# A 128-byte load of W1 rows on ScalarE's queue and a regenerated order, in a fused FFT filter and MLP kernel

## The chip, the cores and the metric

The kernel runs on one core of a Trainium2 chip. The metric is the device time of one execution in microseconds. The kernel before has a median of 148.31 us over three runs, 148.28 to 148.42. All times inside the kernel come from one profiled execution; they count from the start of its span.

## The reference

A batch of one, 2048 rows of 640 values in bf16. The rows are layer-normalized once (xn), and the output is the sum of three terms: x itself, a global filter on xn (a real 2-D FFT, a product with complex weights, the inverse FFT), and a two-layer MLP on xn with a tanh-approximated GELU.

```python
def _A_ref(x, w_r, w_i):
    X = rfft2(x.astype(float32), axes=(-2, -1))
    X = X * (w_r + 1j * w_i)
    return irfft2(X, s=(S, D), axes=(-2, -1)).astype(bfloat16)
def _B_ref(x, w1, b1, w2, b2):
    h = gelu(einsum("bsd,df->bsf", x, w1) + b1)
    return einsum("bsf,fd->bsd", h, w2) + b2
xn = layernorm(x)
return x + _A_ref(xn, A_w_r, A_w_i) + _B_ref(xn, B_w1, B_b1, B_w2, B_b2)
```

S is 2048, D is 640, F (the hidden width) is 1536.

## The kernel before

**Order and synchronization.** The kernel records its work as numbered operations (`Sched.op`), each with what it reads and writes. A long text, `ORDER`, gives for every operation its place and engine (s SyncE, p TensorE, a ScalarE, d VectorE, g GpSimd) and, behind a colon, the buffer slots it takes: `258p:0` is operation 258 on TensorE in slot 0. `arrange` reads that text, and `sync` works out which operation must wait for which, and leaves out waits that follow from others. Each engine then runs its own operations strictly in that order, so an operation that waits holds up everything behind it on its engine. The times written beside the operations (`at=...` for the arrival of a load, in us) are those with which the text was made; the program on the chip contains only the order. An operation keeps the number in which it was recorded, so one more operation shifts the numbers of all later ones by one.

**Loads.** Every load goes through `load`, whose DMA instruction stands at L375. SyncE's queue carries the large ones in this order: the rows of x for chunk 0 and chunk 1 (a chunk is 128 of the 2048 rows, every sixteenth), then W1 in five row blocks of 128 rows by 1536 columns (L433 to L436, 384 KB each; block j holds the weights of the j-th 128 of the 640 inputs) with chunks 2 and 3 of x between the third and the fourth, then the FFT table `gtab` (L437), the other chunks of x in pairs, b2 and W2. ScalarE's queue first loads the table of the square root, then issues the load of b1 (L432), then runs the square root of the first chunk's variance (L489), and loads the table of the GELU (L490). Its later loads come after 21 us.

**Head.** For each chunk VectorE computes statistics (L483, L485), the reciprocal root is made (L489 and L491 for chunk 0, GpSimd at L494 for the others), and VectorE normalizes (L513). Chunks 0 to 3 are transposed by TensorE (L531) and copied out of PSUM to xnT by VectorE and ScalarE (L394, L395); later chunks go through DMA transposes. Until its first input is ready TensorE multiplies zeros (L409, 40 matmuls). The first layer of the MLP begins with chunks 0 and 1 together: six tiles of hidden units (b = 0 to 5, L570 on), each a sum over the five row blocks of W1. In the first three row blocks the two chunks have matmuls of their own, 128 wide, recorded in pairs (two halves of a tile); in the last two they go together, 256 wide. All matmuls have one source line, L383, since a helper issues them; the profile shows these as `ps<-xnT,W`. The copies out of PSUM are likewise in one helper and show as L394 on ScalarE and L395 on VectorE.

TensorE's order in the head is, before the change: five transposes of chunk 0, b1's twelve small products, six pairs on row block 0 (one for each tile), four pairs on row block 1, five transposes of chunk 1, two more pairs on row block 1, one pair on row block 2, and then pairs that need chunk 1.

**Rest.** After the head TensorE runs without a pause the rest of the first layer, the second layer of eight chunks kept for later (`ps<-W,gT`), and between them the stages of the forward FFT, the filter (VectorE at L681) and the inverse FFT. Toward the end it finishes each chunk: VectorE adds the pieces (L778, L787) and the result is stored, or added to the output, by DMA. Evacuations of the FFT stages may be placed on ScalarE or VectorE; `ORDER` says which. The last group of the inverse FFT is 128x640 wide; its two evacuations to `yo` are both on ScalarE (126 to 128 us).

Of the kernel before, what the change touches and what calls it, by code (L numbers as in the profile page):

```python
# [9 lines left out]
ACT = mybir.ActivationFunctionType  # L10
# [4 lines left out]
F = 1536  # L15
# [240 lines left out]
250p 28s 241p 69d 252p 280p 253p 65d 240p 273p 292p 262p 68d 242p 263p 293p 66d 254p 294p 70d 243p 67d 244p 71d 255p 133d 72g 245p 257a 282p 264p 283p 247a 295p 140d:1 284p 256a  # L256
265p 143d 141p:5 296a 144p:2 146d:0 142a 274p 145d 275p 285p 297a 147d 322p:4 246a 301p:7 287a 76d 316p:2 267a 302p 151d:1 149d 328p:5 150d 286a 323p 85d 303a 310p:6 81d 324a 311p
329p 90d 277a 317p 331p:4 73d 312a 325p:7 266a 101d 332p 330a 100d 307p:6 318a 326p 97d 313p:5 333a 98d 314p 327a 138p:0 102d 99d 308p 315a 103d 148d 137p 104g 309a 298p:7 89d 139a
299p 93d 319p:4 5g 6g 194d:1 304p:5 92d 305p 195s 320p 300a 91d 153p:0 94d 196d 321a 152p 95d 572p:6 306a 84d 96g 29a 197s 77d 573p 74d 154a 589p:4 181d:0 75d 590p 183d 182s 78d
30a 591p 185d:0 186d 31a 574p 82d 184s 276a 592p 187d:1 79d 189d 575p 80g 190d 188d 576p 83d 36s 198d:0 199d 577p 37s 86d 114d 593p 578d 192p:0 191p 155d:1 594p 193a 157d 156s  # L260
397p:6 87d 595d 88g 398p 32a 201d:1 373p:7 203d 200d 158s 399a 202d 374p 168d:0 376p:4 113d 375a 169s 170d 377p 159d:0 204p:1 160d 385p:5 115d 171s 117d 205p 162d:0 161d 400p:7
206a 164d 163d 401p 38s 116d 386p 108d 378a 39s 388p:6 118d 119d 105d 387a 120g 40s 403p:4 106d 402a 109d 41s 165p:1 107d 166p 33a 222d:1 42s 404p 220d 389p 405a 43s 224d:0 343p:7
225d 167a 221s 110d 344p 229d:1 226d 346p:5 227d 228d 345a 347p 44s 173d:0 34a 111d 355p:4 172d 112g 223s 390a 177d:0 230p:1 175d 176d 231p 348a 209d:0 356p 174d 334p:6 233a 207d
335p 212d:0 210s 357a 358p:5 211d 232a 216d:1 359p 213d 336a 208s 214d 178p:0 215d 179p 360a 364p:6 180d 35a 45s 217p:3 218p 349p:7 46s 219a 365p 47s 350p 48s 445p:0,0 351a 49s
366a 352p:4 50s 447d 446a 51s 337p:5 353p 442p:0,1 338p 443d 444a 409p:6 339a 460p:0 234g 433p:7 462d:1 461a:0 235g 434p 354a 463p:0 435a 410p 236g 465d 464a 427p:4 411a 237g
471d:0 448p:0,1 466d:1 415p:5 449a 470d 424p:6 467d 450a 428p 416p 469d:1 468d 421p:7 417a 473d:0 425p 472d 429a 484p:0 422p 485d:0 486a:1 430p:5 423a 477p:0 418p:4 478d:2 479a:1
431p 426a 474p:0 379p:7 475d 476a 380p 432a 481s 487p:0 367p:6 489d 488a 419p 483s 490d:1 368p 420a 454p:0,0 491d 381a 480s 494d:0 391p:4 455a 456d 382p:7 482s 383p 495d 451p:0,1
384a 497d:0 492d:1 412p:7 452a 453d 370p:5 369a 371p 493d 511p:0 496d 394p:6 513a:0 512d:1 395p 372a 498p:0 392p 499d:1 500a:2 361p:5 393a 508p:0 413p 510d 509a 340p:4 396a 518d:0
501p:0 414a 362p 503d 502a 341p 626p:6 514d:1 342a 505s 457p:0,1 519d 627p 459d 458a 504s 628p 363a 515d 629p 535p:0 517d:0 608p:4 536a:0 537d:1 630p 507s 516d 532p:0 521d:1 609p
520d 533a 534d 506s 631p 610p 539d:1 525p:0 632d 611p 527a:0 542d:0 612p 526a:1 663p:6 543d 522p:0 538d 613p 523a 664p 614d 524a 529s 665p 544d:1 645p:4 540d:0 666p 528s 541d 545d  # L270
646p 667p 531s 668p 647p 669d 530s 648p 546p:0 700p:6 547a:1 548d:2 649p 736d 650p 701p 651d 549p:0 746d 702p 551a 436p:4 550a 554s 437p 439p:5 438a 553s 703p 440p 704p 441a 552s
705p 682p:4 706d 683p 555s 406p:1 407p 563p:6 408a 564p 692a 565p 684p 566p 556p:0 685p 558d:1 557a 567p 618a 559d:0 582p:0 560d 562d:0 561d 568p 584a:1 583d 569p 686p 655a 687p
585d:0 619p:0 570d:6 586d 571g 599p:6 620a:0 621d 600p 601p 588d:1 656p:0 688d 587d 602p 657a:1 623d:0 579p:4 603p 622d 658a 604p 625d:0 728a 605p 580d:7 693p:0 624d 581g 636p:4
606d:1 695a:0 637p 660d:0 607g 694a 638p 673p:6 633p:0 615p:2 634d:3 639p 640p 616d:6 635g 641p 652p:0 617g 674p 653d:0 675p 659d 654g 642p 729p:0 643d:2 676p 662d:0 731a:1 644g
710p:4 661d 730a 677p 697d:0 670p:0 711p 671d:4 596p:2 678p 696d 672g 712p 597d:6 679p 713p 680d:7 719p:2 698d:1 681g 720p 689p:0 721p 690d:1 714p 699d 691g 737p:6 732d:0 722p 598g
733d 738p 739p 715p 716p 740p 717d:4 723p 718g 707p:0 747p:5 708d:5 741p 748p 734d:0 709g 724p 735d 725p 742p 726d:0 743p 756p:4 749p 744d:6 727g 750p 751p 757p 745s 752p 753p 758p
759p 754d:2 760p 761p 762p 765p:7 755s 766p 763d 767p 768p 769p 764s 770p 771p 772d 773s
"""


# [16 lines left out]
def bass_parallel_sum__spectral_gfnet__dense_activation_gelu__prompt_kernel(  # L297
# [15 lines left out]
    w1v = B_w1.rearrange("(c p) f -> p c f", p=128)  # L313
# [5 lines left out]
    with ExitStack() as es:  # L319
        def sb(name, shape, dtype=BF):  # L320
            return es.enter_context(nc.sbuf_tensor(name, shape, dtype))
# [155 lines left out]
        for c0, n in [(0, 1), (1, 1)] + [(c, 2) for c in range(2, 16, 2)]:  # L477
# [8 lines left out]
            a, b = c0, c0 + n  # L486
            if not c0:
                first = aggr
                K.op([("act", 0.17)], 420, lambda e, _: e.activation(ve[:, 0:1], mv[:, 0, 1:2], ACT.Sqrt, bias=eps[:], scale=1.0), reads=[B_mv, B_eps], writes=[B_ve], hard=queued["act"][:2])  # L489
# [338 lines left out]
```

## Time and profile before

| | us |
|---|---|
| median of three runs | 148.31 |
| the profiled execution | 148.24 |
| its span (first to last instruction) | 146.4 |
| TensorE, matmuls | 142.3 |
| VectorE | 110.6 |
| ScalarE | 76.2 |
| GpSimd | 21.4 |

In the profile PE is TensorE's matmuls, PEld its weight loads (which overlap with the matmuls), DVE is VectorE, ACT is ScalarE, POOL is GpSimd, SP is SyncE; a name with q, such as SPq, is the engine's issue of a DMA. A timeline row gives start, length, engine, source line, operation, output and input, the number of instructions merged into it, and in brackets how long the engine had been idle and who released it. A DMA row gives output and input, queue, count, size, and the time from issue to landing. A row of a table of stretches gives the stretch and its length, the busy time of each engine, the granted clock of TensorE (1.00 is full), the busy share of the 16 DMA engines and the bytes per second that they moved. Where such a table is asked for one engine, it has the columns of that engine alone, and for SyncE, which computes nothing, only clock, share and GB/s.

### The profile page before, as it was taken

The numbers are of one execution on the slowest core, as the hardware profiler recorded it, in microseconds if no ns is written. First come the engines' busy times: TensorE is split into PE (matmuls) and PEld (weight loads), VectorE is DVE, ScalarE is ACT, GpSimd is POOL, SyncE is SP. The second block draws the span as 40 slices with busy tenths as digits, with TensorE's granted clock in tenths as the row PEclk, the third lists the DMA queues.
The fourth block names the chain that finished last, engine by engine and source line by source line (L and its number), as shares of the span: only waits on it lengthen the run. The fifth ranks groups of instructions, "written<-read, shape, count | busy, mean of one in ns | idle before, by whom it ended". The sixth has DMA issues, their size and how long they took to land.

```text
span 146.4 us, 3965 instructions
## 1 busy us (share of the span) xinstructions
PE 142.3 (97%) x1685; PEld 89.3 (61%) x1685; DVE 110.6 (76%) x237; ACT 76.2 (52%) x125; POOL 21.4 (15%) x35
## 2 busy tenths in 40 slices
PE   7899999999999999999999999999999999999992
PEld 7799995655566545445545455555576665655571
DVE  1898999999994459659959999471059995996571
ACT  3517995158786697887678554143445471300000
POOL 1102031211010041000000000000000125526240
PEclk9999999999999999999999999999999999999999
DMA  4999999669999989908300932515300307976685
GB/s 118 322 396 399 348 385 217 161 135 95 183 176 185 206 230 330 358 23 115 67 4 10 118 63 42 117 24 111 69 4 0 45 5 89 118 81 83 81 100 124
DMA packets 27923, 21.00 MB, mean 143 GB/s; under 512 B 20226, under 2 KB 25090, under 8 KB 27779
## 3 DMA queue, kind: packets, MB, share of 16 engines
q1 hardware_dynamic: 24528, 15.03, 43.5%
q0 software_dynamic: 2592, 4.92, 18.3%
q10 hardware_dynamic: 786, 0.82, 2.4%
q8 instruction: 13, 0.21, 0.6%
q14 instruction: 4, 0.02, 0.0%
HBM read 13.54 MB, written 5.24 MB: 128 GB/s over the span
## 4 chain that ended last, share of the span: by engine, by line
PE 94%; DVE 2%; DMA 2%; issue 0%
PE ps L383 93%; DMA X<-in_A_x_dram 2%; DVE stats L483 1%; PE ps L531 1%; DVE T L513 0%; DVE mv L485 0%; DVE W L787 0%; DVE xnT L395 0%; DVE rstd L491 0%; DVE ve L493 0%
## 5 line engine op out<-in xcount | busy, mean ns | idle before, releaser
L383 PE MATMUL ps<-xnT,W 128*128 128x512 bf16 (+2 forms) x336 | 57.7, 320 | 0.1
L383 PE MATMUL ps<-W,gT 128*128 128x512 bf16 (+3 forms) x396 | 57.6, 296 | 0.0
L383 PEld LDWEIGHTS ps<-W,gT 128*128 128x128 bf16 x396 | 30.1, 98 | 22.8 <-issue 1.5
L383 PEld LDWEIGHTS ps<-xnT,W 128*128 128x128 bf16 x336 | 31.6, 114 | 17.3 <-issue 2.2
L614 ACT ACTIVATE gT<-ps,b1col 128x512 bf16<-128x512 f32 (+1 forms) x48 | 28.9, 637 | 6.8 <-PE ps L383 6.6
L794 POOL DMA_DIRECT2D out_dram<-W x14 | 12.2, 902 | 74.0 <-DVE W L787 74.0
L483 DVE BATCH_NORM_STATS2 stats<-X 128x6 f32<-128x320 bf16 x32 | 13.9, 479 | 2.2 <-DMA X<-in_A_x_dram 2.2
L394 ACT ACTIVATE Wf<-ps 128x960 bf16<-128x960 f32 (+1 forms) x9 | 7.6, 880 | 12.0 <-PE ps L383 7.0
L394 ACT ACTIVATE XV<-ps 128x1280 bf16<-128x1280 f32 (+2 forms) x8 | 8.8, 1104 | 7.7 <-PE ps L383 7.7
L681 DVE TENSOR_TENSOR T<-Y,Wf 128x1288 bf16<-128x1288 bf16 x16 | 12.5, 824 | 0.1
L494 POOL TENSOR_TENSOR rstd<-ve,mhalf 128x2 f32<-128x2 f32 (+1 forms) x8 | 6.2, 770 | 33.1 <-DVE ve L493 33.1
L394 ACT ACTIVATE Xb<-ps 128x960 bf16<-128x960 f32 (+1 forms) x7 | 8.0, 1165 | 3.8 <-PE ps L383 3.8
L395 DVE CAST Y<-ps 128x644 bf16<-128x644 f32 x8 | 6.6, 828 | 4.0 <-PE ps L383 3.9
L547 DVE TENSOR_TENSOR T<-T 128x128 bf16<-128x128 bf16 (+1 forms) x32 | 8.5, 320 | 0.1
L394 ACT ACTIVATE T<-ps 128x512 bf16<-128x512 f32 (+1 forms) x14 | 5.4, 442 | 6.0 <-PE ps L383 6.0
L395 DVE CAST Xb<-ps 128x960 bf16<-128x960 f32 (+1 forms) x5 | 5.5, 1110 | 3.8 <-PE ps L383 3.8
L787 DVE TENSOR_TENSOR W<-ps,X 128x640 bf16<-128x640 f32 x7 | 5.7, 822 | 2.4 <-PE ps L383 2.4
L543 DVE TENSOR_TENSOR T<-T 128x640 bf16<-128x640 bf16 x16 | 7.4, 488 | 0.2
L513 DVE TENSOR_SCALAR T<-X,mv,rstd 128x640 bf16<-128x640 bf16 x16 | 6.7, 432 | 1.1 <-POOL rstd L494 1.1
L394 ACT ACTIVATE Y<-ps 128x644 bf16<-128x644 f32 x8 | 5.7, 708 | 3.4 <-PE ps L383 3.4
L383 PE MATMUL ps<-etab,XV 32*128 32x160 bf16 (+1 forms) x128 | 7.2, 232 | 0.0
L383 PE MATMUL ps<-Wf,htab 128*128 128x512 bf16 (+3 forms) x33 | 7.1, 295 | 0.0
(55 smaller groups left out, 127.4 us busy)
## 6 DMA issues: line engine op xcount, KB each, us to landing
out_dram<-in_A_x_dram POOLq DMA_DIRECT2D x4, 640.0 KB, 7.3
X<-in_A_x_dram SPq DMA_DIRECT2D x7, 320.0 KB, 8.8
out_dram<-W POOLq DMA_DIRECT2D x14, 160.0 KB, 3.5
W<-in_B_w_dram SPq DMA_DIRECT2D x5, 384.0 KB, 5.4
W<-in_B_w_dram SPq DMA_DIRECT2D x3, 640.0 KB, 12.4
Wf<-in_A_w_i_dram SPq DMA_DIRECT2D x7, 160.5 KB, 4.0
Wf<-in_A_w_r_dram SPq DMA_DIRECT2D x5, 160.5 KB, 3.5
gtab<-c_G SPq DMA_DIRECT2D x1, 512.0 KB, 7.4
```

The costliest lines, as they stand in the source:

```text
L383: ins = e.matmul(o_, lhsT=lw, rhs=rh, start=st, stop=sp_, skip_group_check=True)
L394: return e.activation(dst(), src(), ACT.Copy, scale=scale)
L395: return e.tensor_copy(dst(), src())
L483: st_ops.append(K.op([("dve", 0.393)], pr, lambda e, _, c=c, h=h: e.bn_stats(stats[:, c, 6 * h:6 * h + 6], view(X, c * D + H2 * h, [[1, H2 ...
L494: K.op([("pool", 0.75)], 400 + pr, lambda e, _, a=a, b=b: e.tensor_tensor(out=rstd[:, a:b], in0=ve[:, a:b], in1=mhalf[:, a:b], op=ALU.pow) ...
L513: o = K.op([("dve", 0.356)], pr, lambda e, _, c=c, n=n, xnv=xnv: e.tensor_scalar(out=xnv(n, 0, [[1, D]]), in0=view(X, c * D, [[1, D]]), sc ...
L543: K.op([("dve", 0.39)], pr, lambda e, _, k=k, op=op, xnv=xnv, x1v=x1v: e.tensor_tensor(out=x1v(H2 * k, [[D, 2], [1, H2]]), in0=xnv(0, 0, [ ...
L547: ring_ops.append(K.op([("dve", 0.333 if w == 128 else 0.136)], pr, lambda e, _, op=op, x1v=x1v, xfv=xfv, o_=o_, o0=o0, o1=o1, w=w: e.tens ...
L614: K.op([("act", act_us(128 * nt, 1) + 0.02)], pr + PRIO["gelu"], lambda e, _, c0=c0, nt=nt, fc=fc, hps=hps: e.activation(gT[:, fc, 128 * c ...
L681: filt_ops.append(K.op([("dve", 0.738)], pr, lambda e, _, k=k, Y=Y, TB=TB, pair=pair: e.tensor_tensor(out=view(TT, TB.slot * 8 * KP + k * ...
L787: K.op([("dve", dve_us(w))], 95, lambda e, _, os_=os_, fps=fps, o0=o0, w=w, xo=xo, base=base: e.tensor_tensor(out=view(W1, OST + os_.slot ...
L794: last.append(K.op([("pool", 0.9)], 450, lambda e, _, c=c, os_=os_: e.dma_start(ov[:, c, :], view(W1, OST + os_.slot * D, [[1, D]]), accum ...
```

## The change

A new load is recorded between b1's and W1's. It reads four bytes each from 32 places of W1: rows 0, 8, ..., 120 of row block 0 and the same rows of row block 1, and puts them in a new 16 by 4 tile, `near`, that nothing reads. It stands on ScalarE's queue behind b1's load, and the square root of L489 is told to come behind it. In SBUF the new tile takes 32 bytes in front of `eps`, so all tiles declared from there on (`eps`, `rstd`, W1, W2, gT, xnT, X and the rest) lie 32 bytes higher.

The noted arrival times change: W1's blocks and chunks 2 and 3 of x by about 0.5 us, `gtab` by 0.8 and the later chunks of x by 0.85 to 1.5.

`ORDER` is replaced as a whole. The operations are the same apart from the new one (number 12, so that all from 12 on are counted one higher). On TensorE the head now runs four pairs on row block 0, one pair on row block 1, two on row block 0, four on row block 1, the transposes of chunk 1, and then pairs on row blocks 2 and 1. 21 evacuations change between ScalarE and VectorE, 11 to VectorE and 10 to ScalarE, among them one of the two last `yo` ones, which goes to VectorE. On VectorE the statistics of chunks 2 and 3 move ahead of three of the small sums of the first pair (L547). SyncE keeps its loads of the first 10 us in the same order; some DMA transposes and filter loads behind 20 us change places among themselves.

```diff
 ORDER = """
-9s 2a 0d 4g 1d 7g 8p:7 3g 11a 10s 12s 13s 14s 15s 54d 55d 16s 17s 56d 60d 57a 18s 58a 59d 121d:1 19s 61d 20s 124p:7 122p:3 62d 52p:4 21s 125a 63d 123d 64g 22s 238p:6 53a 268p:3
-258p:0 278p:1 23s 288p:7 248p:2 126d 259p 24s 279p 239p 269p 132d:0 127p:4 25s 129p:5 249p 128d 289p 130a 290p 131d 26s 291p 261p 271p 270p 136d:0 27s 281p 135d 251p 272p 260p 134d
...
+0d 9s 2a 1d 3g 6g 4g 8p:5 11a 10s 12a 13s 14s 15s 16s 55d 56d 17s 18s 57d 61d 58a 19s 59a 60d 122d:1 20s 62d 21s 125p:4 123p:5 53p:6 63d 22s 64d 124d 65g 5g 126a 54a 23s 269p:3
+249p:7 279p:0 239p:5 270p 259p:1 24s 127d 289p:6 290p 25s 132d:0 26s 280p 240p 250p 128p:4 130p:2 129d 131a 133d 281p 251p 241p 291p 27s 242p 252p 243p 292p 253p 28s 244p 282p 254p
...
 """
...
         mhalf = sb("mhalf", [128, 16], F32)
+        near = sb("near", [16, 4])
         eps = sb("eps", [128, 1], F32)
...
         load(part(gT, 0, 1, 0, [[1, F]]), b1v, B_b1t, 3072, q="act", prio=409, at=3.2)
-        for j, at in enumerate((6.1, 7.05, 8.0, 10.15, 11.1)):
+        load(bass.AP(tensor=near, offset=0, ap=[[4, 16], [2, 2], [1, 2]]), bass.AP(tensor=w1v.tensor, offset=w1v.offset, ap=[[8 * F, 16], [128 * F, 2], [1, 2]]),
+             Buf("near"), 128, q="act", prio=408, at=3.6)
+        for j, at in enumerate((5.6, 6.6, 7.55, 9.6, 10.55)):
             if j == 3:
-                load_x(2, 2, next(pr), at=9.15)
+                load_x(2, 2, next(pr), at=8.6)
             load(W1[:, F * j:F * j + F], w1v[:, j, :], B_w1s[j], 393216, prio=next(pr), at=at)
-        load(gtab[:], const["G"], B_g, 524288, prio=next(pr), at=12.9)
-        for c, at in zip(range(4, 16, 2), (14.6, 15.45, 16.25, 17.1, 17.9, 18.75)):
+        load(gtab[:], const["G"], B_g, 524288, prio=next(pr), at=12.1)
+        for c, at in zip(range(4, 16, 2), (13.1, 14.6, 15.45, 16.25, 17.1, 17.9)):
             load_x(c, 2, next(pr), at=at)
...
-                K.op([("act", 0.17)], 420, lambda e, _: e.activation(ve[:, 0:1], mv[:, 0, 1:2], ACT.Sqrt, bias=eps[:], scale=1.0), reads=[B_mv, B_eps], writes=[B_ve], hard=queued["act"][:2])
+                K.op([("act", 0.17)], 420, lambda e, _: e.activation(ve[:, 0:1], mv[:, 0, 1:2], ACT.Sqrt, bias=eps[:], scale=1.0), reads=[B_mv, B_eps], writes=[B_ve], hard=queued["act"][:3])
```

More of the change, by code (lines that the diff above doesn't have):

```diff
@@ new lines @@
+7g 89g 595p 156d:1 194a 202d 201d 158d 203d 157s 398p:7 374p:6 375p 159s 205p:0 376a 596d 169d:0 171d 399p 401p:4 206p 172s 160d:0 402p 389p:5 170s 386p:6 118d 109d 161d 110d
+162d:1 116d 165d 119d 107d 120d 121g 38s 400a 403a 36a 207a 387p 39s 164d 106d 163d 108d 221d:1 377p:7 40s 404p:4 378p 390p 41s 388a 391a 379a 223d 42s 166p:0 405p 167p 335p:6 168a
+111d 225d:0 226d 112d 230d:0 229d 227d 228d 336p 347p:5 174d:0 113g 406a 173d 232p:0 337a 208d:0 231p 359p:7 175d:0 176d 210d 178d 177d 234a 43s 224s 44s 45s 209s 222s 360p 348p
@@ new lines @@
+611p 522d:1 633d 521d 535a 534a 612p 613p 526p:0 614p 527a:1 528d:0 664p:6 523p:0 665p 543d:0 615d 544d 524a 666p 646p:4 525a 529s 647p 546d:1 545d 539d:1 530s 540d 667p 542d:0
+541d 668p 648p 669p 649p 670d 531s 532s 650p 547p:0 548d:1 549a:2 701p:6 651p 652d 550p:0 702p 747d 551a 552d 703p 440p:5 441p 704p 554s 705p 407p:4 706p 442a 553s 556s 737d 707d
+437p:5 408p 438p 555s 409a 564p:6 439a 565p 566p 693a 683p:4 684p 567p 685p 557p:0 559d:0 558a 686p 568p 619a 561d:0 560d 583p:0 562d:1 563d 687p 569p 585a:0 729a 584d 570p 688p
@@ L278 @@
+682g 708p:6 724p 717p 709d:5 718d:2 739p 725p 733d 719g 710g 726p 736d:1 735d 727d:3 728g 740p 748p:4 749p 741p 742p 743p 757p:7 744p 745d:7 746s 750p 758p 751p 759p 752p 753p 754p
+760p 761p 762p 766p:2 755d:6 767p 763p 768p 756s 769p 770p 764d 771p 772p 765s 773d 774s
 """
```

36 lines of the change are left out of this document (14 added, 22 removed).

## The prediction

> **What bounds the kernel now.** I read the page's first part, then the chain of waits in order of time, then the head of the kernel.
>
> ```profile
> PE 142.3 (97%) x1685; PEld 89.3 (61%) x1685; DVE 110.6 (76%) x237; ACT 76.2 (52%) x125; POOL 21.4 (15%) x35
> ```
> ```profile
> 0.74 2.34 DMA X<-in_A_x_dram
> ...
> 3.10 0.90 DVE stats L483 x2
> ...
> 6.08 0.21 DVE xnT L395
> 6.29 0.05 issue
> 6.33 1.45 PE ps L383 x20
> 7.78 0.28 PE ps L531 x5
> 8.06 4.95 PE ps L383 x70
> 13.01 0.61 PE ps L531 x10
> 13.62 130.04 PE ps L383 x1477
> 143.65 0.03 issue
> 143.68 0.33 DVE W L787
> ```
>
> The chain has two parts. Up to 6.33 us it is a latency chain: the first 128 rows of x land, VectorE takes their statistics and normalizes them, TensorE transposes, VectorE copies the first half of xnT out. From 6.33 us to the end it is TensorE in program order. A change can pay only by starting that stream sooner or by taking a wait out of it, and costs what it adds to either. The table of stretches says how little there is to take out later:
>
> ```profile
> 0.00:20.00 20.00, 18.61 (x226) 17.78 (x227) 15.40 (x50) 12.15 (x28) 2.79 (x11) 1.00 0.91 325
> 20.00:40.00 20.00, 20.00 (x148) 12.38 (x147) 19.67 (x67) 12.04 (x18) 3.27 (x8) 1.00 0.89 180
> 40.00:60.00 20.00, 20.00 (x253) 11.47 (x251) 14.05 (x26) 15.69 (x22) 3.14 (x5) 1.00 1.00 232
> ...
> 120.00:140.00 20.00, 20.00 (x159) 11.61 (x158) 14.88 (x24) 2.67 (x4) 9.76 (x12) 1.00 0.74 87
> ```
>
> First numbers in a row: length, then busy time of PE, PEld, DVE, ACT, POOL. The clock is 1.00 throughout. Busy is no proof of full pitch, because ends of matmuls are modelled, so in the head I count starts instead. The question is whether W1 is late there:
>
> ```profile
> 1.67 0.43 SPq L375 DMA_DIRECT2D W<-in_B_w_dram  x1
> W<-in_B_w_dram SPq DMA_DIRECT2D x1, 384.0 KB, 4.0
> ...
> 2.13 0.43 SPq L375 DMA_DIRECT2D W<-in_B_w_dram  x1
> W<-in_B_w_dram SPq DMA_DIRECT2D x1, 384.0 KB, 5.0
> ...
> 2.61 0.43 SPq L375 DMA_DIRECT2D W<-in_B_w_dram  x1
> W<-in_B_w_dram SPq DMA_DIRECT2D x1, 384.0 KB, 5.4
> ```
> ```profile
> 6.32:6.98 0.66, 0.65 (x12) 1.00 1.05 340
> ```
> ```profile
> 6.33 1.06 PE L383 MATMUL ps<-xnT,W 128*128 128x128 bf16 x13
> ```
> ```profile
> 7.62 0.44 PE L531 MATMUL ps<-ident,T 128*128 128x128 bf16 x5
> ```
>
> Issue plus time to landing: W1's row blocks 0, 1, 2 are there at 5.67, 7.13 and 8.01 us. Block 0 is ahead of 6.33, so it is not on the path. Five transposes last 0.44 us with 0.22 us for one (0.45 busy is five overlapping): a pitch of (0.44 - 0.22) / 4 = 0.055 us. The first twelve matmuls, all on block 0, start between 6.33 and 6.98, one each 0.055. By 7.20 (the next row ends there) only one more has started, where 15 or 16 would have at that pitch: the thirteenth needs block 1 and began when it landed, about 0.14 us late (7.13 against 6.33 + 12 x 0.055 = 6.99). That wait is all that W1 costs now. The waits name another in the head:
>
> ```profile
> 14.20 1.89 PEld L383 LDWEIGHTS ps<-xnT,W 128*128 128x128 bf16 x18 [0.19 <-DVE xnT L395]
> ```
>
> **The change, part by part.**
>
> *The small load, as work.* One DMA issue on ScalarE's queue, directly behind the b1 load:
>
> ```profile
> 0.74 1.28 ACT L401 ACT_TABLE_LOAD   x1 [0.74 <-PEq L813]
> 0.77 0.53 ACTq L375 DMA_DIRECT2D gT<-in_B_b_dram  x1
> 4.27 0.29 ACT L489 ACTIVATE ve<-mv,eps 128x1 f32<-128x1 f32 x1 [2.25 <-DVE mv L485]
> ```
>
> It goes out at 0.77 + 0.53 = 1.30 and, at b1's 0.53, is done at 1.83. Queued behind it on ScalarE is the square root at L489, which waits for VectorE until 4.27; its idle 2.25 us are the cover. Cost 0, and 0.53 if that cover were gone. Nothing waits for the load's data. SP's order of loads is untouched up to 10 us.
>
> *The small load, as company for other transfers.*
>
> ```profile
> 1.50:1.75 0.25, 1.00 0.03 12
> 2.75:3.25 0.50, 1.00 1.01 299
> 3.25:4.25 1.00, 1.00 0.78 209
> 4.25:5.25 1.00, 1.00 1.00 289
> 5.25:6.25 1.00, 1.00 0.96 369
> ```
>
> Last column GB/s, the one before it the busy share of the DMA engines. 12 GB/s over 0.25 us is 3 KB: b1's packet, the first traffic, at most 0.98 us behind its issue. So the small load's packets come at 1.30 + 0.73 to 0.98, 2.0 to 2.3 us, ahead of W1's. The dip at 3.25 to 4.25 is where W1's first blocks begin: at the rate of 5.25 to 6.25, 1 - 209/369 = 0.43 us of transfer is lost there and 1 - 289/369 = 0.22 us in the next one. If that is the price of touching W1's rows the first time, and the small load pays it early, block 1 lands 0.43 (first dip alone) to 0.65 us sooner: 6.70 to 6.48. If not, it lands at 7.13; and 32 packets of 4 bytes, two for each of 16 engines, can also take time from the x loads beside them. The trace has no such load, so the bounds on block 1 are 0 and -0.65. I take -0.43: the dip stands exactly where W1 starts.
>
> *The new order at the head.* Before, TensorE does six pairs on block 0 (twelve matmuls), then block 1. The new order does four pairs, then one pair of block 1. The wait for it comes four matmuls sooner: at 6.33 + 8 x 0.055 = 6.77, plus some 0.03 that the first weights cost. Landing at 6.70, it costs nothing, and 0.14 us is saved. Landing at 7.13, the wait is 0.33 instead of 0.14: +0.19. So the reordering spends what the load is to bring; without 0.33 us of help it loses. Behind the transposes of x's second 128 rows stand eight matmuls instead of six before the one that needs their copy, and ahead of the wait at 14.20 there is one 128-wide pair more: 2 x 0.055 = 0.11 us more cover at each. The 0.19 quoted is idle time of the weight loads, which run ahead; of it and the smaller wait at the copy I count 0.08 as gained (bounds 0 and 0.25).
>
> *The new order after that.* The matmuls are the same 1685. 21 evacuations change engine, 11 to VectorE and 10 to ScalarE, so net one copy more on VectorE. Their prices:
>
> ```profile
> L394 ACT ACTIVATE Wf<-ps x9: 698/966/971, 107.6 to 127.0; 128x960 bf16<-128x960 f32 x6, 128x640 bf16<-128x640 f32 x3
> ...
> L395 DVE CAST Wf<-ps x3: 825/1152/1152, 107.6 to 113.4; 128x960 bf16<-128x960 f32 x2, 128x640 bf16<-128x640 f32 x1
> ```
>
> A 128x640 copy is 0.70 us on ScalarE, 0.83 on VectorE. What hides it is TensorE's other queued work; unhidden, one such copy costs up to 0.83. VectorE has 0.33 us idle in 20 to 40. The most exposed one is the last group's (128x640, now on VectorE at about 127 us), where eight matmuls stand between the work that fills the banks and the one that reuses them. PE is busy for 20.00 of 20 in every stretch there: 0, with bounds 0 and +0.83. The new tile also moves those declared behind it by 32 bytes; no row prices that: 0 both ways.
>
> *Sum.* -0.14 - 0.08 = -0.22 on the profiled execution's 148.24 (146.4 of span, 1.84 around it): 148.02. The median of the runs shown is 0.07 higher, 148.31; the same step there gives **148.1**.
>
> **Rivals.**
>
> *The small load holds up x's first rows (slower).* The first x load is issued at 0.74 and takes 2.3:
>
> ```profile
> X<-in_A_x_dram SPq DMA_DIRECT2D x1, 160.0 KB, 2.3
> ```
>
> It lands at 3.04 to 3.08, so its last packets run just when the small load's arrive, on the same engines. A load is there only when its slowest engine is done: from 3.25 to 5.25 about 209 + 289 = 498 KB moved, more than block 0's 393 KB, and yet block 0 landed at 5.67. If an engine spends on a cold packet what the dips cost, 0.43 to 0.65 us, from 2.2 on, the x load lands up to about 3.6, and 6.33 moves one for one. Against it: most of the 160 KB is through by then. Price +0.5, less the W1 wait and its neighbour (-0.22): 148.31 + 0.28 = 148.6. It decides from an x landing later than about 3.3. The Trainium skill ("DMA: Bandwidth & Descriptors", section "Queues, rings and completion order") speaks for this rival: a semaphore increment is a strongly ordered write that lands behind every earlier write of that engine, across its queues. No run here shows it yet.
>
> *The load does not do what it says.* The dip may be how loaded HBM behaves and not a first touch; then block 1 stays at 7.13: +0.19 - 0.08 = +0.11, 148.4. For it: the dip goes on in 4.25 to 5.25, beyond block 0. Against it: the x load's own start and the 299 before 3.25 have no such dip. The same page, section "Latency and other measured facts", gives HBM reads 0.2 us on average and 2 us at high load; by that the dip would be load, and the time this rival's.
>
> *Every head wait goes.* The 0.14, all of the 0.19 and some 0.06 more: -0.39, 147.9. For it: later x loads also gain from a shorter dip. Against it: VectorE at 13 us, not the loads, made the 0.19.
>
> *A late copy shows.* 0.3 of the 0.83 unhidden, with the forecast's gain: 148.4.
>
> **How the numbers follow.** Forecast 0.45, its own range 147.9 to 148.3. Held-up x 0.2, no help 0.15, every wait gone 0.12, late copy 0.08. About 0.2% (0.3 us) is what a measurement here tells from no change: below 148.01 is faster, above 148.61 slower. Faster: a third of the forecast (0.16), nearly all of "every wait" (0.11) and 0.03 from elsewhere, 0.30. Slower: half of held-up x (0.10), a quarter of "no help" and half of the late copy (0.04 each), 0.02 elsewhere, 0.20. Same 0.50. Range 147.8 to 148.7: down to just past every wait gone, up to held-up x with 0.1 over.
>
> **What would show it.** Right: W1's block 1 lands by 6.8, GB/s in 3.25 to 4.25 nears 300, the first x load stays at 3.1, the first xnT matmul at 6.33, and no gap after the eighth. Wrong: block 1 at 7.1 with a gap of 0.3 after eight matmuls; x landing at 3.3 or later with the whole stream shifted; or a PE wait for a copy behind 14 us, above all at 127, which would put the cost in the order and not in the load.

## The result and the profile after

The changed kernel takes 150.02 us (median of six runs), the kernel before in the same session 148.29 (148.26 to 148.42): a ratio of 1.0104, interval 1.0061 to 1.0147. One of the six runs (152.09 us at a granted clock of 0.989) and one of a later kernel (154.91 at 0.978) fell in a slower state of the chip: the ratios and the lowest and highest times in this document leave them out, the medians count them. The change is slower by about 1%, and its other five runs spread from 149.22 to 150.61. The prediction, 148.1 with a range up to 148.7, was wrong in sign and in size.

The profiled execution took 149.45 us, 1.21 over that of before. Its span is 147.6 against 146.4, so all of the difference lies inside the span. The chain of waits of the changed kernel, in order of time (start, length, what; `...` stands for pieces left out, above all the long stretch of VectorE work between 8 and 26 us):

```profile
2.13 5.08 DMA W<-in_B_w_dram
...
7.26 0.97 PE ps L384 x14
...
26.04 3.89 DMA xnT<-T
...
30.02 114.83 PE ps L384 x1329
...
144.88 0.33 DVE W L790
```

Before, this chain was TensorE in program order from 6.33 us on. Now it passes through W1's row block 1 (landed at 2.13 + 5.08 = 7.21, with TensorE released at 7.26), then through VectorE, and, at 26.04, through a DMA transpose of xnT which TensorE waits for until 30.02. The timeline of TensorE shows the same two places (start, length, engine, line, operation, count, and in brackets the idle time before and its releaser):

```profile
6.39 0.64 PE L384 MATMUL ps<-xnT,W 128*128 128x128 bf16 x8
7.26 0.97 PE L384 MATMUL ps<-xnT,W 128*128 128x128 bf16 x14 [0.23 <-DMA W<-in_B_w_dram]
...
22.11 5.60 PE L384 MATMUL ps<-W,gT 128*128 128x512 bf16 x40
...
30.02 1.24 PE L384 MATMUL ps<-xnT,W 128*128 128x512 bf16 x5 [0.67 <-DMA xnT<-T]
```

and here are the corresponding rows of the kernel before:

```profile
21.89 6.14 PE L383 MATMUL ps<-W,gT 128*128 128x512 bf16 x44
...
28.97 3.40 PE L383 MATMUL ps<-xnT,W 128*128 128x512 bf16 x15
```

Between those two places both kernels run the same second-layer matmuls and `gtab` products. From the first of them to the first 512-wide xnT matmul before needs 28.97 - 21.89 = 7.08 us and after 30.02 - 22.11 = 7.91. So the difference of 144.88 - 143.68 = 1.20 us at VectorE's last addition is made of three pieces: 0.22 at 22 us (22.11 against 21.89), 0.83 at the wait for xnT, and 0.15 in all that follows (144.88 - 30.02 against 143.68 - 28.97). The head, which the prediction was about, holds a small piece, and with the other sign: the forecast's sum had TensorE 0.22 us earlier from there on, and it is 0.22 later.

Now the loads at the head, after (rows: issue, then DMA with size and time from issue to landing):

```profile
0.74 0.40 SPq L376 DMA_DIRECT2D X<-in_A_x_dram  x1
X<-in_A_x_dram SPq DMA_DIRECT2D x1, 160.0 KB, 2.3
...
1.34 0.37 ACTq L376 DMA_DIRECT2D near<-in_B_w_dram  x1
near<-in_B_w_dram ACTq DMA_DIRECT2D x1, 0.1 KB, 2.3
```
```profile
3.25:4.25 1.00, 1.00 0.82 200
```

The first rows of x land at 0.74 + 2.3 = 3.04, as before. The small load lands at 1.34 + 2.3 = 3.64. Block 1 of W1, at 7.21, had landed at 7.13 before. The stretch from 3.25 to 4.25 moves 200 GB/s, where it was 209: the dip stays.

The last thing to look at is the four DMA transposes that make xnT's chunks 8 to 11, the chunks of that 512-wide matmul. Before, then after; each row of SyncE's queue is one or four issues:

```profile
20.64 5.96 SPq L522 DMA_TRANSPOSE xnT<-T  x4
...
25.32 1.28 SPq L522 DMA_TRANSPOSE xnT<-T  x1
xnT<-T SPq DMA_TRANSPOSE x1, 2.4
```
```profile
21.64 5.70 SPq L525 DMA_TRANSPOSE xnT<-T  x4
```

Two things differ. The first transpose goes out 1.00 us later (the last one, at 26.04 in the chain, 0.72), and the last one takes 3.89 us from issue to landing where it took 2.4. Before, the last landed at 25.32 + 2.4 = 27.72, 1.25 us ahead of its use at 28.97. Now it lands at 26.04 + 3.89 = 29.93, and TensorE, which would have been there at 22.11 + 7.08 = 29.19, waits. What else moves data in that stretch is seen on ScalarE's queue, before and after:

```profile
28.64 0.59 ACTq L375 DMA_DIRECT2D Wf<-in_A_w_r_dram  x1
```
```profile
23.11 1.22 ACTq L376 DMA_DIRECT2D Wf<-in_A_w_r_dram  x2
24.39 0.64 ACTq L376 DMA_DIRECT2D Wf<-in_A_w_r_dram  x1
```

The new order puts three loads of the filter w_r (160.5, 10 and 150.5 KB) between 23.1 and 25.0 us, into the middle of the transposes; the old order has the first of them at 28.64, when these four transposes are through. This was in the new `ORDER` text (33a and 34a directly behind 32a on ScalarE, 35a one ScalarE operation later), and the prediction did not name it; the section on the change speaks of filter loads only where it speaks of SyncE.

### The profile page after: what moved, and what is told of

Read it like the earlier page. It is cut to its first block, busy times and chain, and to the rows that moved or that the text cites. A ratio compares the mean times of both kernels' runs of the same rounds, so it can differ in the third digit from the quotient of the medians.

```text
span 147.6 us, 3968 instructions
## 1 busy us (share of the span) xinstructions
PE 143.0 (97%) x1685; PEld 89.5 (61%) x1685; DVE 111.3 (75%) x240; ACT 75.4 (51%) x122; POOL 21.5 (15%) x35
## 4 chain that ended last, share of the span: by engine, by line
PE 79%; DVE 10%; DMA 6%; SPq 1%; POOL 1%; issue 1%
PE ps L384 78%; DVE stats L486 5%; DMA W<-in_B_w_dram 3%; DMA xnT<-T 3%; DVE T L516 2%; DVE T L546 1%; POOL rstd L497 1%; DVE T L550 1%; SPq L376 1%; DVE xnT L396 1%; SPq L525 0%; DVE mv L488 0%; DVE W L790 0%; DVE ve L496 0%; PE ps L534 0%
## 5 line engine op out<-in xcount | busy, mean ns | idle before, releaser
L384 PE MATMUL ps<-W,gT 128*128 128x128 bf16 (+3 forms) x396 | 57.9, 296 | 0.0
L617 ACT ACTIVATE gT<-ps,b1col 128x512 bf16<-128x512 f32 (+1 forms) x48 | 28.6, 638 | 11.4 <-PE ps L384 11.1
L395 ACT ACTIVATE Wf<-ps 128x960 bf16<-128x960 f32 (+1 forms) x7 | 6.1, 893 | 14.6 <-PE ps L384 12.7
L395 ACT ACTIVATE Xb<-ps 128x960 bf16<-128x960 f32 (+1 forms) x8 | 8.7, 1130 | 3.0 <-PE ps L384 3.0
L396 DVE CAST Wf<-ps 128x960 bf16<-128x960 f32 (+1 forms) x5 | 5.1, 1023 | 5.5 <-PE ps L384 5.4
L395 ACT ACTIVATE Y<-ps 128x644 bf16<-128x644 f32 x10 | 6.8, 705 | 4.2 <-PE ps L384 4.2
L396 DVE CAST Y<-ps 128x644 bf16<-128x644 f32 x6 | 5.0, 828 | 4.9 <-PE ps L384 4.9
L396 DVE CAST Xb<-ps 128x960 bf16<-128x960 f32 (+1 forms) x4 | 4.7, 1166 | 3.8 <-PE ps L384 3.8
L688 DVE TENSOR_TENSOR Z<-T 128x644 bf16<-128x644 bf16 x16 | 7.1, 489 | 0.1
L749 DVE TENSOR_TENSOR Wf<-Wf 128x960 bf16<-128x960 bf16 (+1 forms) x12 | 6.9, 598 | 0.3
## 6 DMA issues: line engine op xcount, KB each, us to landing
Wf<-in_A_w_i_dram SPq DMA_DIRECT2D x7, 160.5 KB, 4.0
Wf<-in_A_w_r_dram SPq DMA_DIRECT2D x5, 160.5 KB, 4.4
```

The source lines that it names most:

```text
L384: ins = e.matmul(o_, lhsT=lw, rhs=rh, start=st, stop=sp_, skip_group_check=True)
L395: return e.activation(dst(), src(), ACT.Copy, scale=scale)
L396: return e.tensor_copy(dst(), src())
L617: K.op([("act", act_us(128 * nt, 1) + 0.02)], pr + PRIO["gelu"], lambda e, _, c0=c0, nt=nt, fc=fc, hps=hps: e.activation(gT[:, fc, 128 * c ...
L688: K.op([("dve", 0.402)], pr, lambda e, _, TB=TB, Z=Z, r=r, op=op: e.tensor_tensor(out=view(Zb, Z.slot * 4 * KP + r * KP, [[2 * KP, 2], [1, ...
```

## The experiments

Eleven other kernels and the changed one again, each measured beside the kernel before on the same chip. The ratio is to that kernel in the same session, with its 95% interval; its medians in the three sessions of experiments were 148.41, 148.25 and 148.49, over 23 to 29 runs that spread over 0.5 to 1.4 us.

| kernel | median, us | lowest to highest | ratio |
|---|---|---|---|
| changed kernel | 150.02 | 149.22 to 150.61 | 1.0104 [1.0061, 1.0147] |
| changed kernel again | 149.80 | 149.42 to 150.49 | 1.0091 [1.0065, 1.0118] |
| tile alone | 148.33 | 148.09 to 148.63 | 0.9994 [0.9981, 1.0008] |
| small load, old order | 148.24 | 148.06 to 148.87 | 0.9989 [0.9973, 1.0004] |
| small load first, old order | 148.24 | 148.00 to 149.02 | 1.0007 [0.9995, 1.0019] |
| block 1 asked for earlier, old order | 148.33 | 148.17 to 149.37 | 1.0016 [1.0002, 1.0029] |
| filter loads early, old order | 149.16 | 148.71 to 149.80 | 1.0072 [1.0054, 1.0090] |
| new order, small load late | 150.42 | 149.36 to 150.90 | 1.0123 [1.0093, 1.0153] |
| new order, small load first | 150.70 | 149.70 to 151.13 | 1.0119 [1.0088, 1.0150] |
| new order, filter loads late and together | 149.65 | 149.48 to 150.46 | 1.0110 [1.0093, 1.0128] |
| new order, filter loads spread | 148.56 | 148.16 to 148.84 | 1.0002 [0.9986, 1.0018] |
| the same, transposes begun as early as before | 148.81 | 148.41 to 149.22 | 1.0020 [1.0006, 1.0034] |
| the same, small load first as well | 148.59 | 148.38 to 148.88 | 1.0012 [0.9998, 1.0025] |

### The change in its three parts

First question: is it the load, the order, or the tile that shifts addresses? One kernel has the load in the old order, one the new order with the load moved out of the head, one the tile alone; the changed kernel was run again for scale. In the cuts below `...` stands for lines left out, and where the small load is in the kernel the numbers from 12 on are one higher, as in the change.

The small load in the old order:

```diff
+        near = sb("near", [16, 4])
...
+        load(bass.AP(tensor=near, offset=0, ap=[[4, 16], [2, 2], [1, 2]]), bass.AP(tensor=w1v.tensor, offset=w1v.offset, ap=[[8 * F, 16], [128 * F, 2], [1, 2]]),
+             Buf("near"), 128, q="act", prio=408, at=3.6)
...
-9s 2a 0d 4g 1d 7g 8p:7 3g 11a 10s
+9s 2a 0d 4g 1d 7g 8p:7 3g 11a 12a 10s
```

> The kernel before with the tile and the small load added, and its own order kept. Order theory (the new order makes the 1.04% loss, the load is idle company): 148.3 within 0.2, first W1 block-1 matmul waits at most 0.3 us in place of 0.14, no wait of TensorE for an xnT transpose. Load theory (the small load's packets, which in the changed kernel ran with W1's first ones, hold up W1 and x and through them everything behind): 149.0 or more. Clock theory (TensorE reaches full rate at 5.99 us in place of 4.38, by chance of each execution): times spread over 1 us as in the changed kernel.

Measured 148.24, ratio 0.9989 [0.9973, 1.0004]. The load costs nothing, and if it brings something, it is under 0.3%.

The new order with the small load moved behind 20 us, just ahead of the first FFT table:

```diff
-0d 9s 2a 1d 3g 6g 4g 8p:5 11a 10s 12a 13s 14s
+0d 9s 2a 1d 3g 6g 4g 8p:5 11a 10s 13s 14s
```

> The changed kernel with the small load moved behind the head on ScalarE's queue (just ahead of the etab load, about 22 us), so that it can do nothing for W1 or x. Order theory: 149.2 to 150.6 as the changed kernel, a gap of 0.3 to 0.4 us after the first eight W1 matmuls, and a wait for an xnT transpose near 29 us. Load theory: 148.4 or less.

Measured 150.42, ratio 1.0123 [1.0093, 1.0153]: the whole loss without the small load in the head. The gap after eight matmuls that was expected with it did not come: block 1 landed at 6.50, and the first 22 matmuls ran in 1.42 us. (The moved load has a price of its own here, 0.38 us on ScalarE's queue at 21.18, just ahead of the loads in question.) In its view of waits (engine, group, releaser, us in total, times, longest) the wait for xnT stands first:

```profile
PE ps L380 <- DMA xnT<-T: 1.0, 1, 1.0
```

The tile alone, which shifts the later tiles by 32 bytes:

```diff
+        near = sb("near", [16, 4])
```

> The kernel before with only the unused 16x4 tile declared, so that all later tiles lie 32 bytes higher; no load, same order. Order theory and load theory: 148.3 within 0.1. Address theory (the shift slows DMA transposes or copies): 148.7 or more, with xnT transposes that take longer from issue to landing than 3.7 us in the median.

Measured 148.33, ratio 0.9994 [0.9981, 1.0008]: nothing, as predicted.

The changed kernel once more, unchanged:

> The changed kernel unchanged, for a second profile and the spread of its times. Order theory: two waits again, after eight W1 matmuls (0.3 to 0.4) and for an xnT transpose near 29 us (0.5 to 2), and the spread of 149.2 to 150.6 lies in the second one. Clock theory: the time follows the moment at which TensorE reaches full rate, 1 us of delay there for each us of the total's spread.

Measured 149.80, ratio 1.0091 [1.0065, 1.0118]. Its chain starts through chunks 2 and 3 of x and not through W1, and from 9.07 us on it has the same form, with a transpose that takes 4.73 us from issue to landing instead of 3.89:

```profile
25.67 4.73 DMA xnT<-T
```

So the loss is the order's, and it goes through the transposes. It differs from one execution to another as the transposes' time does. Four profiled executions of the new order with its early filter loads show this (the last is of a kernel described further below):

| execution | last of the four transposes, issue to landing | first 512-wide xnT matmul at | time |
|---|---|---|---|
| kernel before | 2.4 | 28.97 | 148.24 |
| changed kernel | 3.89 | 30.02 | 149.45 |
| changed kernel again | 4.73 | 30.49 | 149.91 |
| new order, small load late | 5.1 | 31.24 | 150.63 |
| new order, small load first | 5.9 | 31.72 | 151.13 |

In the four lower rows the time minus that start is 119.39 to 119.43 us: what the wait adds goes to the end one for one.

The expectations named a clock theory too: that the time follows the moment at which TensorE reaches its full rate. The traces do not bear it out. The 40 matmuls on zeros at the start took 4.45 us in the changed kernel (4.01 before), but also 4.45 in the kernel with the tile alone, at 148.31 us, and 3.67 in the slowest of the four executions above.

### What of the order costs: the filter loads

Two explanations were open for the late xnT: the transposes begin 1.0 us later, or the filter loads lengthen them. The loads were first moved in both orders.

The old order with the first three filter loads right behind the last FFT table, as the new order has them:

```diff
-30a 591p 185d:0 186d 31a 574p 82d
+30a 591p 185d:0 186d 31a 32a 33a 34a 574p 82d
```

> The kernel before with the same three filter loads moved early on ScalarE's queue, right behind the ntab load (about 23 us), and nothing else. Collision theory: the four transposes land 1.5 to 2.5 us later than 27.76 and TensorE, which needs them at 28.97, waits 0.3 to 1.3: 148.7 to 149.7. Start theory: 148.4 within 0.2.

Measured 149.16, ratio 1.0072 [1.0054, 1.0090]: this alone costs some two thirds of what the change costs. In its profile TensorE is held in another place. The GELU's row in the kernel before, then here the rows of ScalarE and of TensorE:

```profile
23.39 0.48 ACT L596 ACTIVATE gT<-ps,b1col 128x256 bf16<-128x256 f32 x1
```
```profile
23.68 1.90 ACTq L371 DMA_DIRECT2D Wf<-in_A_w_r_dram  x3
25.62 0.47 ACT L592 ACTIVATE gT<-ps,b1col 128x256 bf16<-128x256 f32 x1 [2.23 <-issue]
```
```profile
26.15 2.35 PE L379 MATMUL ps<-W,gT 128*128 128x512 bf16 x16 [0.41 <-ACT gT L592]
```

Three issues take 1.90 us of ScalarE, a GELU behind them starts at 25.62, where in the kernel before that GELU ran at 23.39, and TensorE waits for its output. A DMA issue on ScalarE's queue is no idle company: what stands behind it on ScalarE waits some 0.6 us for each of these. (An operation that is already running is not held: before, an issue from 22.61 to 23.06 falls inside an activation that runs from 22.27 to 23.51.)

The transposes are lengthened in this order too, as the collision theory had it. The last of the four:

```profile
25.27 1.30 SPq L518 DMA_TRANSPOSE xnT<-T  x1
xnT<-T SPq DMA_TRANSPOSE x1, 4.1
```

It takes 4.1 us where it took 2.4, and lands at 25.27 + 4.1 = 29.37 instead of 27.72. TensorE, half a microsecond late through the GELU, comes to it at 29.47; at before's 28.97 it would have had to wait. So by these figures the one cost hides the other in this execution.

The new order with those loads moved behind the transposes, but still together, directly ahead of the fourth:

```diff
-278a 591p 185s 32a 575p 576p 592p 33a 34a 183s
+278a 591p 185s 32a 575p 576p 592p 183s
...
-38s 400a 403a 36a 207a
+38s 400a 403a 33a 34a 35a 36a 207a
```

> The changed kernel with one thing of its order undone: the three filter loads that the new order puts on ScalarE's queue at 23.1 to 24.4 us, beside the DMA transposes of xnT chunks 8 to 11, go back behind them (just ahead of ScalarE's fourth filter load). Collision theory (those loads slow the four transposes, which landed at 29.93 in place of 27.76, and TensorE ran dry at 29.1): the last of the four lands by 28.6, the wait near 29 us is gone, 148.3 to 148.8. Start theory (the transposes are late because VectorE normalizes their chunks later and SyncE begins at 21.64 in place of 20.64): the wait stays at 0.7 or more, 149.2 or more.

Measured 149.65, ratio 1.0110 [1.0093, 1.0128], in neither expected range. The part on the transposes came as the collision theory had it: the last one goes out at 25.82, takes 2.7 us and lands at 28.5, and the wait for xnT is gone from the view of waits. Yet little is won, because the four issues now hold ScalarE at another place where TensorE depends on it:

```profile
33.27 2.94 ACTq L372 DMA_DIRECT2D Wf<-in_A_w_r_dram  x4
36.26 1.24 ACT L391 ACTIVATE XV<-ps 128x1280 bf16<-128x1280 f32 x1 [2.31 <-issue]
```
```profile
PE ps L380 <- ACT XV L391: 0.5, 1, 0.5
```

(The view of waits has 0.6 us more on TensorE that it puts to no releaser.) TensorE needs 116.29 us from the first 512-wide xnT matmul (29.27) to VectorE's last addition, where the changed kernel needs 114.86. So this run showed the second price of the loads, and its time could not decide on the first. The next one moved them, and the fourth, singly, each to about the time at which the old order has it:

```diff
-278a 591p 185s 32a 575p 576p 592p 33a 34a 183s
+278a 591p 185s 32a 575p 576p 592p 183s
...
-194a 202d
+194a 33a 202d
...
-379a 223d
+379a 34a 223d
...
-337a 208d:0
+337a 35a 208d:0
...
-38s 400a 403a 36a 207a
+38s 400a 403a 207a
...
-361a 233a
+361a 36a 233a
```

> The changed kernel, with the loads of w_r's halves and the one after them on ScalarE's queue put back one at a time to where the old order has them (near 29, 36, 39 and 44 us), and nothing else. Theory 'collision' (the filter loads lengthen the four transposes of xnT's chunks 8 to 11, and the three issues in a row hold ScalarE): last of the four transposes lands by 28.9, no wait for xnT at 29, no wait for gT: 148.4 to 148.8 us. Theory 'late start' (the transposes begin 1.0 us later, the loads are idle company): the last lands at 28.9 or later, a wait for xnT stays: 149.0 us or more.

Measured 148.56, ratio 1.0002 [0.9986, 1.0018]. The whole loss is gone. Everything else of the new order is still in this kernel, the late start of the transposes too. SyncE's last transpose of the four, then TensorE:

```profile
26.28 1.28 SPq L521 DMA_TRANSPOSE xnT<-T  x1
xnT<-T SPq DMA_TRANSPOSE x1, 2.6
```
```profile
21.89 5.60 PE L380 MATMUL ps<-W,gT 128*128 128x512 bf16 x40
...
29.02 1.24 PE L380 MATMUL ps<-xnT,W 128*128 128x512 bf16 x5
```

The last transpose goes out at 26.28, even later than in the changed kernel (26.04), but it takes 2.6 us instead of 3.89, lands at 28.9, and TensorE is not held: 29.02 is 7.13 us behind 21.89, against 7.08 before. The DMA queues between 23 and 28 us show what was taken away. The first fence is of the changed kernel, the second of the spread one; q1 carries the transposes and SyncE's loads, q10 is ScalarE's queue (packets, MB, share of the 16 engines' time):

```profile
q1 hardware_dynamic: 1590, 0.41, 64.5%
q10 hardware_dynamic: 639, 0.49, 56.9%
...
xnT<-T SPq DMA_TRANSPOSE x4, 4.7
```
```profile
q1 hardware_dynamic: 2214, 0.55, 75.1%
q10 hardware_dynamic: 311, 0.15, 28.2%
...
xnT<-T SPq DMA_TRANSPOSE x4, 2.9
```

With q10's share halved, q1 gets 0.55 MB through instead of 0.41, and the median time of a transpose falls from 4.7 to 2.9 us. The profile counts both queues' time on the same 16 engines. Over all fourteen profiles the last of the four transposes took 2.4 to 3.0 us from issue to landing in the nine without the early filter loads, and 3.9 to 5.9 in the five with them, in either order.

### Whether the late start costs

The spread kernel with the first part of the order undone too: chunk 10's normalization is made, and waited for, before chunk 11's.

```diff
-104d 140a 105g 92d 95d 149d
+104d 91d 94d 149d 195d:1 92d 95d 96d 197d 86d 140a 105g
...
-87d 198s 30a
+87d 196s 30a
...
-82d 196s 590p:4
+82d 198s 590p:4
```

> The kernel with the filter loads spread, and with the late start undone too: SyncE waits for chunk 10's norm before chunk 11's, as in the old order, and VectorE makes chunk 10's norm before the next two chunks' statistics. Theory that both parts of the order cost: SP's first of the four transposes goes out near 20.7, the last lands by 27.9, no wait at 29: 148.2 to 148.5. Theory that something else in the new order costs: still 148.8 or more.

```profile
20.72 6.19 SPq L521 DMA_TRANSPOSE xnT<-T  x4
```

The transposes begin at 20.72 again, as before. The time is 148.81, ratio 1.0020 [1.0006, 1.0034], not better than the spread kernel's, and by the letter of what was expected it lies with "something else". The last transpose lands at 25.62 + 2.7 = 28.3 (27.9 was expected) and is not waited for. So undoing the late start won nothing; it had used up slack (1.25 us between landing and use before, 0.1 in the spread kernel). The profiled execution (149.05, against 148.44 of the spread kernel) differs elsewhere: W1's block 1 landed at 7.31, TensorE ends its first 22 matmuls 0.26 us later than in the spread kernel, is 0.30 later at 22 us, and needs 0.31 more from 29.33 to the end without a wait that the view names; that last part stays unexplained.

### What a wait at the head is worth

The prediction took it that a wait taken out of TensorE's stream at 7 us comes out of the end. Four runs bear on that. The old order with one matmul pair on block 1 moved to where the new order has it, after eight matmuls:

```diff
-268p:3 258p:0 278p:1 23s 288p:7 248p:2 126d 259p 24s 279p 239p 269p
+268p:3 258p:0 278p:1 23s 269p 288p:7 248p:2 126d 259p 24s 279p 239p
```

> The kernel before with one pair of matmuls moved: the first pair on W1's row block 1 comes after four pairs on block 0 in place of six, as in the new order. It prices the head wait by itself. If a wait there goes through to the end: a gap of 0.3 us after eight matmuls in place of 0.14 after twelve, 148.5 to 148.6 against 148.4. If a later wait absorbs it (the one for the xnT copy at 14.2): 148.4 within 0.1.

Measured 148.33, ratio 1.0016 [1.0002, 1.0029]. Its profile shows twenty matmuls in 1.31 us, where the chain of before has them in 1.45: no long gap, with no small load either. Block 1 landed at 6.59 in this execution, ahead of 6.25 + 8 x 0.055 = 6.69 where it is asked for, so the run has no wait there and cannot price one.

```profile
6.25 1.31 PE L379 MATMUL ps<-xnT,W 128*128 128x128 bf16 x20
```

The small load ahead of b1's on ScalarE's queue, in the old order:

```diff
-9s 2a 0d 4g 1d 7g 8p:7 3g 11a 10s
+9s 2a 0d 4g 1d 7g 8p:7 3g 12a 11a 10s
```

> The kernel before with the small load ahead of b1's on ScalarE's queue, so that it is issued at 0.77 in place of 1.34 and its packets come about 0.6 us sooner, ahead of W1's first ones and not beside them as in the changed kernel (2.85 us and later). First-touch theory: row blocks 0 and 1 of W1 land 0.4 us or more sooner than 5.7 and 7.1, the head wait of 0.14 goes, 148.1 to 148.25. Loaded-HBM theory: blocks 0 and 1 within 0.2 of those landings, 148.4. Held-up-x theory: the first x load lands at 3.3 or later and the time is 148.6 or more.

Here the small load's packets come ahead of W1's, as the prediction had wanted. The trace has 48 of them, where the prediction counted 32; with b1's two they are through by 2.8 us; from 2.25 to 2.8 ScalarE's queue has

```profile
q10 hardware_dynamic: 50, 0.00, 6.4%
```

while the changed kernel has no row for q10 in that stretch, and its packets follow from 2.8 to 3.25:

```profile
q10 hardware_dynamic: 48, 0.00, 6.0%
```

Block 1 landed at 2.13 + 4.2 = 6.33, and the gap at the head is gone, as the first-touch theory had it (twenty matmuls in 1.31 us, 1.45 before):

```profile
2.13 0.43 SPq L372 DMA_DIRECT2D W<-in_B_w_dram  x1
W<-in_B_w_dram SPq DMA_DIRECT2D x1, 384.0 KB, 4.2
```
```profile
6.27 1.31 PE ps L380 x20
...
143.46 0.33 DVE W L786
```

That execution ends 0.22 us earlier than the profiled one of before, but the median over eleven runs is 148.24 and the ratio 1.0007 [0.9995, 1.0019]: no gain that can be measured (the kernel before had 148.25 in that session). Nor do the landings show that the load is the reason. Block 1 landed between 6.5 and 7.1 us in the five profiles without a small load in the head, and between 6.3 and 7.3 in the nine with one; with it first on its queue, at 6.33, 6.64 and 7.13.

The same in the new order:

```diff
-0d 9s 2a 1d 3g 6g 4g 8p:5 11a 10s 12a 13s
+0d 9s 2a 1d 3g 6g 4g 8p:5 12a 11a 10s 13s
```

> The changed kernel with the small load one place earlier, ahead of x's block 1 on ScalarE's queue, and nothing else. Theory 'order': W1's block 1 lands by 6.6, the gap after the first eight matmuls goes (0.39 in the changed kernel), and the wait for xnT near 29 stays or grows by the same: 149.0 to 150.0 us. Theory 'the head is what costs': the gain at the head stays to the end: 148.6 or less.

(The load that it passes is b1's; x's loads are on SyncE's queue.) Measured 150.70, ratio 1.0119 [1.0088, 1.0150], above the 149.0 to 150.0 of the theory 'order', whose missing gap and longer wait for xnT it shows (block 1 landed at 6.64). TensorE's rows and part of the chain:

```profile
6.42 1.42 PE L380 MATMUL ps<-xnT,W 128*128 128x128 bf16 x22
...
22.12 5.60 PE L380 MATMUL ps<-W,gT 128*128 128x512 bf16 x40
...
31.72 0.59 PE L380 MATMUL ps<-xnT,W 128*128 128x512 bf16 x2 [2.35 <-DMA xnT<-T]
```
```profile
3.09 5.95 DMA X<-in_A_x_dram
...
9.06 1.67 DVE stats L482 x4
```

The first 22 matmuls take 1.42 us; in the changed kernel they take 7.26 + 0.97 - 6.39 = 1.84. So 0.42 us is won at the head, and at 22.12 all of it is lost again (22.11 in the changed kernel). The chain says why: it does not pass through W1 any more but through chunks 2 and 3 of x, which land at 3.09 + 5.95 = 9.04, and VectorE's work on them. And the wait for xnT is 2.35 us here, since the transposes took longer still (3.89 in the changed kernel, 5.9 here for the last):

```profile
25.72 1.31 SPq L521 DMA_TRANSPOSE xnT<-T  x1
xnT<-T SPq DMA_TRANSPOSE x1, 5.9
```

Last, all three mended together, as the candidate for a kernel better than both:

```diff
-0d 9s 2a 1d 3g 6g 4g 8p:5 11a 10s 12a 13s
+0d 9s 2a 1d 3g 6g 4g 8p:5 12a 11a 10s 13s
...
-104d 140a 105g 92d 95d 149d
+104d 91d 94d 149d 195d:1 92d 95d 96d 197d 86d 140a 105g
...
-592p 33a 34a 183s
+592p 183s
```

> Filter loads spread, start undone, and the small load first on ScalarE's queue. If head and order add up: the gap after eight matmuls gone and no wait at 29, 147.9 to 148.3. If what is won at the head is waited for later, as with the small load first in the old order (148.24): 148.2 to 148.5.

Measured 148.59, ratio 1.0012 [0.9998, 1.0025], above both expected ranges. In its profile there is no wait at 29, but nothing is won at the head either: block 1 lands at 7.13, and the first 22 matmuls take 1.67 us. No version beats the kernel before by more than can be measured; the nearest is the small load in the old order, 0.9989 [0.9973, 1.0004].

## Why the prediction was wrong

**The step that failed** is "The new order after that", with its "PE is busy for 20.00 of 20 in every stretch there: 0, with bounds 0 and +0.83". It measured slack in the profile of the old order and used it for the new one. That TensorE was busy throughout before says only that every input came in time in that order. What had to be asked is how early each input came, and whether the new order keeps it. For the last xnT transpose the slack was 28.97 - 27.72 = 1.25 us. The new order takes 0.72 by the later issue and 3.89 - 2.4 = 1.49 by its longer way, beside the filter loads, 2.21 in all, against 1.25 and the 0.22 by which TensorE itself comes later: 0.74 late, and 0.09 more from landing (29.93) to start (30.02) make the 0.83 measured. The step looked at 21 copies that changed engine, each at most 0.83 us, and not at the DMAs that changed places: the three filter loads on ScalarE's queue, at 23.1 to 25.0 us instead of 28.6 and later. With these and the load after them moved back one by one the time was 148.56, a ratio of 1.0002. That the upper bound is the same figure as the wait is chance.

**"The small load, as work": 0.** Right. It is issued at 1.34 (forecast 1.30) under ScalarE's wait, and the old order with it measured 148.24.

**"Its packets come at 2.0 to 2.3 us, ahead of W1's".** Wrong. Behind b1's load they came between 2.8 and 3.25, together with W1's first. Ahead of b1's they come before 2.8. For the changed kernel the rival "The load does not do what it says" held: block 1 at 7.21 (that rival had 7.13, the forecast 6.70), the dip at 200 GB/s.

**The dip as "the price of touching W1's rows the first time", -0.43.** Not borne out. The stretch from 3.25 to 4.25 us moved 160 to 270 GB/s in the five profiles without a small load in the head, and 178 to 249 in the nine with one. The dip differs between executions by as much as the effect that was read from it, and one execution was not enough to price it. The Trainium skill ("DMA: Bandwidth & Descriptors", section "Latency and other measured facts") lets the latency of HBM reads depend on the load. The dip fits with that as well, but these runs do not show its cause.

**"The new order at the head": the wait comes four matmuls sooner.** Right in form: in the changed kernel the gap stands after eight matmuls, as the list of signs had it. It was 7.26 - 6.39 - 8 x 0.055 = 0.43 us, where that list had 0.3 for a landing at 7.1. Whether it comes depends on block 1's landing, which varies by execution.

**The sum's premise, -0.14 - 0.08 out of the end.** Wrong in the new order with its early filter loads, where 0.42 us won at the head were gone by 22 us: another chain, through x's chunks 2 and 3 and VectorE, lay right behind the one that was shortened. "Every head wait goes" at 147.9 falls with it. In the old order the gain showed in one profile and not in the median, and in the spread kernels, where that other chain does not hold TensorE, a head that ended 0.26 us later was still 0.31 later at 29 us.

**"Held-up x".** It did not occur in the changed kernel, where x's first rows landed at 3.04. With the small load first on its queue the first statistics of x began at 3.04, 3.19 and 3.22 in three executions, against 3.03 to 3.11 in the other eleven, so a delay of some 0.1 us is possible there; none came near the 0.5 of that rival. Whether the rule of the Trainium skill that was set beside it ("DMA: Bandwidth & Descriptors", section "Queues, rings and completion order") has a part in this, no run here shows.

**"A late copy shows" at about 127 us.** No. From the first 512-wide xnT matmul to VectorE's last addition the changed kernel needs 114.86 us, before 114.71.

**The 32-byte shift: 0.** Right: the tile alone measured 148.33.

The sign that the list named last, "a PE wait for a copy behind 14 us ... would put the cost in the order and not in the load", pointed to the right part of the change, with a DMA in the copy's place.

**What stays open.** Why the same transposes beside the same loads take from 3.9 to 5.9 us in five executions. How the old order's early loads cost 0.72% in the median was read from one profile, the fastest of its runs (148.71), where the held GELU came first and hid the late transposes. Moving the filter loads to another engine's queue was not tried, nor was moving only one of the three.

## What to carry to other kernels

When an order is replaced as a whole, compare the issue times of its DMAs, not only the instructions that compute: list for each transfer that TensorE will wait on when it lands and when it is used, and ask of each moved load whose engines it shares in that interval. A bounding engine that is busy all the time tells you nothing of how much slack its inputs have. A wait taken out at the head is worth no more than the distance to the next chain behind it.

## What the runs showed of the hardware

- Three loads on ScalarE's queue (321 KB) beside four DMA transposes on SyncE's lengthened the transposes: the last took 2.4 to 3.0 us from issue to landing in nine executions without them, 3.9 to 5.9 in five with them.
- DMA issues on ScalarE's queue held the compute behind them on ScalarE: three in a row took 1.90 us, four 2.94, and the activation behind them started after them, 2.2 to 2.3 us after ScalarE's last work. An activation already running went on beside an issue (22.27 to 23.51 beside 22.61 to 23.06, before).
- The load of 128 bytes from 32 places took 2.3 us from issue to landing in the changed kernel, as long as 160 KB of x beside it. Nearly all its packets ran before 2.8 us where it was first on its queue (three executions), after 2.8 us where it was second (six).
- Between executions W1's row block 1 landed at 6.3 to 7.3 us, with the small load or without.
